# A third result group's last stage moved behind the last block's sums, and the last half's copies shared by two engines

## The chip, the cores and the metric

The kernel runs on one core of one Trainium2 chip. The metric is the device time of one execution in microseconds (us). The engines named here are TensorE (PE in the profile; its weight loads are listed apart as PEld), VectorE (DVE), ScalarE (ACT), GpSimd (POOL) and SyncE (SP), which only issues transfers here. TensorE writes its results to PSUM, from where ScalarE or VectorE copy them to SBUF.

## The reference

Two long convolutions over a sequence of 2048 steps and 448 channels are computed and mixed by a gate. Cut to what matters:

```python
# A: state-space model; K is a kernel of 2048 taps for each channel
P = jnp.exp(logdA[:, :, None] * l[None, None, :])
K = jnp.einsum("dn,dnl,dn->dl", Cc, P, dB).real
y = irfft(rfft(up) * rfft(Kp))[:, :, :L]        # causal convolution
a = y + u * Dskip
# B: a short convolution (4 taps), times v, then a long one
kv = k_shift * v
b = q * (irfft(rfft(kv) * rfft(ssm_k)) + kv * ssm_D)   # q is u as well
# gate
g = sigmoid((x * gate_w).sum(-1, keepdims=True))
return g * a + (1 - g) * b
```

The sum over the 256 modes of each channel that gives K, and the convolutions, are most of the work.

## The kernel before

The channels are cut in four groups (112 columns in all, 28 in a group, NC). Each convolution is a transform in stages, done with matmuls: *spread* (stage C), *transform* (stage 2), a pointwise product of the two transforms (*products*, or *last* for the last group), then *stage_a* and *stage_b* back. The kernel K of the A groups is built in eight blocks, two to a group: VectorE builds tables TQ and TP of powers, TensorE sums them over the modes (224 matmuls into `pk`), and `gather` and `spread` bring the sums into the form that the transform needs.

The copy functions:

```python
    def evac(dst, src, i=0):
        return nc.scalar.copy(dst, src)

    def evac_two(dst, src, i=0):
        if i == 0:
            nc.scalar.copy(dst, src)
        else:
            V.tensor_copy(dst, src)
```

The stages that the end of the kernel uses:

```python
def spread(nc, psum, W, zs, cols, groups, evac, room=8, tag="ps", at=0):
    for whs in groups:
        pt = psum.tile([P, room, 128], f32, name="ps_c", tag=tag)
        for i, wh in enumerate(whs):
            x = cols(wh)
            for r in range(2):
                nc.tensor.matmul(pt[64 * r:64 * r + 64, i, :], lhsT=x, rhs=W[:, 128 * r:128 * r + 128], start=True, stop=True,
                                 tile_position=(0, 64 * r))
        n = len(whs)
        evac(zs[:].rearrange("p k (g c) -> p (k g) c", g=4)[:, :, at + whs[0]:at + whs[0] + n], pt[:, 0:n].rearrange("p i kg -> p kg i"))
# ...
def transform_half(nc, psum, W, zs, evac, half):
    for kk in range(2):
        pt = psum.tile([P, 2, 512], f32, name="ps_2", tag="ps")
        for i in range(16):
            k = 16 * kk + i
            nc.tensor.matmul(pt[:, i // 8, (i % 8) * 56:(i % 8 + 1) * 56], lhsT=W[:, k].rearrange("p r s -> p (r s)"),
                             rhs=half_of(zs, k, k + 1, half), start=True, stop=True)
        for i in range(2):
            k0 = 16 * kk + 8 * i
            evac(half_of(zs, k0, k0 + 8, half), pt[:, i, 0:448].rearrange("p (k c) -> p k c", c=CB), i)


def stage_a_half(nc, psum, U, R, terms, evac, half):
    for j in range(half * CB, half * CB + CB, 7):
        pt = psum.tile([P, 8, 128], f32, name="ps_a", tag="ps")
        for i in range(7):
            for n, t in enumerate(terms):
                nc.tensor.matmul(pt[:, i, :], lhsT=t[:].rearrange("p k (g c) -> p (k g) c", g=4)[:, :, j + i],
                                 rhs=R[:, 128 * n:128 * n + 128], start=(n == 0), stop=(n == 1))
        evac(U[:, :, :, j:j + 7].rearrange("p r b c -> p (r b) c"), pt[:, 0:7].rearrange("p i rb -> p rb i"))
# ...
def stage_b(nc, psum, G, U, consume, banks=2):
    n = 16 * banks
    for b0 in range(0, 64, n):
        pt = psum.tile([P, banks, 512], f32, name="ps_b", tag="ps")
        for i in range(n):
            b = b0 + i
            o = pt[:, i // 16, (i % 16) * NC:(i % 16 + 1) * NC]
            for r in range(2):
                nc.tensor.matmul(o, lhsT=G[:, b, r].rearrange("p g a -> p (g a)"), rhs=U[:, r, b], start=(r == 0), stop=(r == 1))
        consume(b0, n, pt[:, :, 0:448])
```

`pt` with the tag "ps" is one of three PSUM tiles of two banks each. The end of a block of K, where the sums stand, and the gathering:

```python
# ... KGen.block: tables TQ and TP on VectorE ...
        q512 = mult([TQ[:, 18:19]], 512)
        p64 = mult([TP[:, 0:4]], 64)
        add(TQ, 20, q512)
        add(TP, 8, p64)
        p64 = mult([TP[:, 4:8]], 64)
        back(8, 16)
        add(TP, 12, p64)
        back(0, 8)
        self.last = chain[0]
        with self.tc.high_priority(offset=100000):
            pt = self.pk[:, 0:448].rearrange("p (n b) -> p n b", b=32)
            for hw in range(CB):
                for hf in range(2):
                    for c in range(2):
                        for g in range(4):
                            m = (hf * 4 + g) * CB + hw
                            r0 = TP[:, 0, c, m:m + 1]
                            rhs = bass.AP(r0.tensor, r0.offset, [list(r0.ap[0]), [32 * M + (1 - 2 * c) * M, 2], [2 * M, 16]])
                            nc.tensor.matmul(pt[32 * g:32 * g + NQ, hw, :].rearrange("p (i j) -> p i j", i=2),
                                             lhsT=TQ[:, :, c, m], rhs=rhs, start=(hf == 0 and c == 0),
                                             stop=(hf == 1 and c == 1), tile_position=(0, 32 * g))
            S = self.pool.tile([P, 32, CB], bf16, name="kg_S")
            self.summed = evac(S[:], pt.rearrange("p n b -> p b n"))
# ... KGen.gather: 57 small matmuls in two halves; each half is copied with
#     evac to KT, and both halves use the same PSUM bank ...
```

A block with its spread, and what happens to a group's result:

```python
    def block(j):
        H = j // 2
        if j and j % 2 == 0:
            tb.chunk(H, kg.mid)
        if KA[H] is None:
            KA[H] = qt([P, 32, 4 * NC], "zsK")
        S = kg.block(j, evac, kvl if j == 0 else None)
        with tc.high_priority(offset=100):
            KT = kg.gather(j, S, evac)
            at = (j % 2) * CB
            cols = lambda c: KT[:, :, c]
            if j >= NBLK - 2:
                spread(nc, psum, WcK, KA[H], cols, [range(0, 7), range(7, 14)], evac, at=at)
            else:
                spread(nc, psk, WcK, KA[H], cols, [range(0, 4), range(4, 8), range(8, 11), range(11, 14)], evac, 4, "ps_g", at)
# ...
    def epilogue_A(H):
        def consume(b0, n, pt):
            t = kgp.tile([P, 32, NC], bf16, name="ept")[:, 0:n]
            V.tensor_tensor(out=t.rearrange("p (i b) c -> p i b c", b=16), in0=pt.rearrange("p i (b c) -> p i b c", b=16),
                            in1=gt[:, b0:b0 + n].rearrange("p (i b) -> p i b", b=16).unsqueeze(3).to_broadcast([P, n // 16, 16, NC]), op=ALU.mult)
            V.tensor_tensor(out=window(b0, n, H), in0=t, in1=window(b0, n, H), op=ALU.add)
            if H == NQG - 1:
                store(b0, n, 0, 112)
        return consume

    y2 = []

    def hold_y(H):
        y2.append(hqt([P, 64, NC], "y2"))

        def consume(b0, n, pt):
            evac(y2[0][:, b0:b0 + n].rearrange("p (i b) c -> p i (b c)", b=16), pt)
        return consume

    def mix_y(H):
        for b0 in (0, 32):
            y = y2[0][:, b0:b0 + 32]
            yp = y.rearrange("p b (n t) -> p b n t", t=2)
            V.tensor_tensor(out=yp, in0=yp, in1=gb[:, b0:b0 + 32].unsqueeze(2).to_broadcast([P, 32, NC // 2, 2]), op=ALU.mult)
            V.tensor_tensor(out=window(b0, 32, H), in0=y, in1=window(b0, 32, H), op=ALU.add)
```

One step of the main sequence, and the end of the program:

```python
    def step(c, n, j):
        kind, H = n
        if kind == "B":
            KB[H] = spread_in(skc.pop(H))
            XB[H] = spread_in(kv_cols(H))
        else:
            XA[H] = spread_in(u_cols(H))
        with tc.high_priority(offset=300000):
            U = stage_a(nc, psum, qp, R, terms[c], evac)
        if kind == "B":
            transform(nc, psum, W2, KB[H], evac)
            transform(nc, psum, W2, XB[H], evac)
        else:
            transform(nc, psum, W2, XA[H], evac)
        with tc.high_priority(offset=200000):
            stage_b(nc, psum, G, U, (hold_y if c == ("A", NQG - 2) else epilogue_A if c[0] == "A" else epilogue_B)(c[1]))
        if kind == "B" and H + 1 < NQG:
            skc[H + 1] = sk_cols(H + 1)
        block(j)
        if kind == "B":
            with tc.high_priority(offset=200000):
                terms[n] = products(nc, *swapped(KB[H], kg.summed), XB[H])
        else:
            XA[H] = swapped(XA[H], kg.summed)
        if kind == "A" and H < NQG - 1:
            transform(nc, psum, W2, KA[H], evac)
            with tc.high_priority(offset=200000):
                terms[n] = products(nc, *XA[H], KA[H])
# ...
    for l in range(0, 112, 8):
        nc.tensor.matmul(pg[:], lhsT=ones[:], rhs=ug[:, :, l:l + 8], start=(l == 0), stop=(l == 104))
    gt = wp.tile([P, 64], f32, name="gt")
    V.tensor_reduce(out=gt[:], in_=pg[:], op=ALU.add, axis=mybir.AxisListType.X)
    nc.scalar.activation(gt[:], gt[:], ACT.Sigmoid)
    gb = wp.tile([P, 64, 2], bf16, name="gb")
    V.tensor_copy(gb[:], gt[:].unsqueeze(2).to_broadcast([P, 64, 2]))
    og = wp.tile([P, 64, 2], bf16, name="og")
    V.tensor_scalar(out=og[:], in0=gt[:].unsqueeze(2).to_broadcast([P, 64, 2]), scalar1=-1.0, scalar2=1.0, op0=ALU.mult, op1=ALU.add)
    pairs = lambda t: t[:].rearrange("p b (n t) -> p b n t", t=2)
    V.tensor_tensor(out=pairs(ug), in0=pairs(uu), in1=og[:].unsqueeze(2).to_broadcast([P, 64, 56, 2]), op=ALU.mult)

    seq = [("B", 0), ("B", 1), ("B", 2), ("A", 0), ("B", 3), ("A", 1), ("A", 2), ("A", 3)]
    for j in range(NBLK - 1):
        step(seq[j], seq[j + 1], j)

    U = qt([P, 2, 64, NC], "U")

    def last(half):
        for k0 in (0, 16):
            for t in XA[3][::-1]:
                V.tensor_tensor(out=half_of(t, k0, k0 + 16, half), in0=half_of(t, k0, k0 + 16, half), in1=half_of(KA[3], k0, k0 + 16, half), op=ALU.mult)

    transform_half(nc, psum, W2, KA[3], evac, 0)
    last(0)
    block(NBLK - 1)
    transform_half(nc, psum, W2, KA[3], evac_two, 1)
    stage_a_half(nc, psum, U, R, XA[3], evac, 0)
    last(1)
    mix_y(NQG - 2)
    stage_a_half(nc, psum, U, R, XA[3], evac, 1)
    stage_b(nc, psum, G, U, epilogue_A(3), 1)
```

`tc.high_priority` and the order of the program decide how a scheduler puts the instructions of one engine in order; that order is fixed when the kernel is built. `swapped` issues the transfer that writes a copy `zsS` of `zs` with its two halves of partitions exchanged.

## Time and profile before

| | before |
|---|---|
| time, median of 3 | 325.49 us (325.31 to 325.81) |
| span of the profiled execution | 323.5 us |
| VectorE busy | 277.2 us (86%) |
| ScalarE busy | 243.2 us (75%) |
| TensorE busy, matmuls / weight loads | 225.5 us (70%) / 197.4 us (61%) |
| mean granted TensorE clock | 0.8 |
| last stage B begins | 308.08 us |
| last instruction of VectorE ends | 313.6 us |

The profile is of one execution. A line of the timeline has the start (us from the span's start), the length in us, the engine, the line of the kernel, the operation, what it writes and reads, the shapes, and how many instructions are merged in it; in brackets stands the time that the engine was idle before it and what ended that. The chain of work that ended last is followed back from the last instruction, at each step to what released it; "issue" there is time in which an engine waited for nothing that the profile shows. L565 is the line of the function `evac`, L569 and L571 are those of `evac_two`, so the tile's name tells which copy it is. The granted clock is a share of full speed.

### The profile page before, as it was taken

To read this page: it belongs to the slowest core of one execution; us is meant where nothing else is said; L and a number is where in the kernel's file an instruction comes from. 1 tells how busy PE (TensorE), PEld (TensorE's weight loads), DVE (VectorE), ACT (ScalarE), POOL (GpSimd) and SP (SyncE) were. 2 spreads that over 40 slices of the span, in tenths; PEclk is the share of its full clock that TensorE was granted. 3 is DMA by queue.
4 is the path that set the end of the run, shared out by engine and by line. 5 is a ranking of instruction groups with operands and counts; after the bars stand their busy time and mean duration, and the time that the engine had idled before them with its cause. 6 is when DMAs were issued, how large, how long until landed. Compare 5 with 4: busy or idle time off the path is not lost.

```text
span 323.5 us, 11944 instructions
## 1 busy us (share of the span) xinstructions
PE 225.5 (70%) x5286; PEld 197.4 (61%) x5286; DVE 277.2 (86%) x571; ACT 243.2 (75%) x395; POOL 34.6 (11%) x129
## 2 busy tenths in 40 slices
PE   0498617737278678699997857999774779966740
PEld 0144607237167568588886846998674678865740
DVE  7999999967999899979999998988999889942450
ACT  3655888779991799998989999689989474936600
POOL 9400002912000009000000000000000000000000
PEclk9999855796758767967997975899998559995765
DMA  6889999730000530050040015004000500040048
GB/s 129 137 188 152 165 164 168 239 59 0 2 0 4 117 57 3 5 158 2 4 102 19 4 45 116 3 4 97 22 2 4 115 3 4 12 108 2 2 91 140
DMA packets 53740, 21.41 MB, mean 66 GB/s; under 512 B 49080, under 2 KB 52024, under 8 KB 53688
## 3 DMA queue, kind: packets, MB, share of 16 engines
q1 hardware_dynamic: 48936, 19.47, 31.6%
q10 hardware_dynamic: 4560, 1.15, 2.0%
q8 instruction: 41, 0.67, 0.9%
q14 instruction: 11, 0.09, 0.1%
q0 software_dynamic: 192, 0.03, 0.1%
HBM read 10.09 MB, written 3.21 MB: 41 GB/s over the span
## 4 chain that ended last, share of the span: by engine, by line
ACT 39%; PE 26%; SPq 14%; DVE 9%; POOL 4%; issue 3%; DMA 3%; ACTq 0%; DVEq 0%; POOLq 0%
ACT zs L565 12%; PE ps_b L279 7%; PE pk L371 6%; ACT ET L481 6%; ACT U L565 5%; ACT zsK L565 5%; PE ps_c L215 5%; SPq L634 4%; POOL skraw L592 4%; PE ps L227 3%; SPq L587 3%; PE ps_a L265 3%; ACT ET L493 3%; SPq L631 2%; ACT ET L511 2%
## 5 line engine op out<-in xcount | busy, mean ns | idle before, releaser
L565 ACT CAST zs<-ps_c 128x1024 bf16<-128x1024 f32 (+1 forms) x48 | 42.5, 940 | 4.8 <-PE ps_c L215 4.7
L227 PEld LDWEIGHTS <-s_W 128*128 128x128 bf16 x480 | 34.4, 118 | 16.7 <-issue 14.2
L318 DVE TENSOR_TENSOR kg_P<-kg_TQ,ET 128x896 bf16<-128x896 bf16 (+1 forms) x64 | 43.8, 705 | 0.3
L565 ACT CAST zs<-ps 128x896 bf16<-128x896 f32 x48 | 41.4, 929 | 1.6 <-PE ps L227 1.5
L227 PE MATMUL ps<-zs,s_W 128*128 128x112 bf16 x384 | 32.2, 252 | 12.2 <-ACT zs L565 6.3
L371 PE MATMUL pk<-kg_TP,kg_TQ 128*21 128x32 bf16 x1792 | 30.3, 238 | 8.5 <-issue 6.3
L371 PEld LDWEIGHTS <-kg_TQ 128*21 128x21 bf16 x1792 | 27.8, 121 | 10.3 <-issue 9.6
L265 PE MATMUL ps_a<-sa_R,zs 128*128 128x128 bf16 x196 | 29.0, 240 | 6.8 <-ACT U L565 4.5
L592 POOL TENSOR_TENSOR skraw<-skraw,dB 128x28 bf16<-128x28 bf16 x4 | 23.3, 5816 | 94.9 <-DMA skraw<-in_B_ssm_k_dram 94.9
L565 ACT CAST U<-ps_a 128x1024 bf16<-128x1024 f32 (+2 forms) x32 | 29.3, 947 | 3.5 <-PE ps_a L253 1.8
L318 DVE TENSOR_TENSOR kg_P<-kg_TP,ET 128x1792 bf16<-128x1792 bf16 (+1 forms) x32 | 30.8, 963 | 0.0
L279 PEld LDWEIGHTS <-sb_G 128*128 128x128 bf16 x1024 | 27.9, 99 | 3.9 <-issue 3.6
L279 PE MATMUL ps_b<-U,sb_G 128*128 128x28 bf16 x1024 | 28.1, 179 | 2.9 <-ACT U L565 1.3
L265 PEld LDWEIGHTS <-zsS 128*128 128x128 bf16 x196 | 26.2, 153 | 5.2 <-issue 5.2
L265 PE MATMUL ps_a<-sa_R,zsS 128*128 128x128 bf16 x196 | 28.5, 239 | 0.0
L265 PEld LDWEIGHTS <-zs 128*128 128x128 bf16 x196 | 26.2, 152 | 2.6 <-DVE zs L286 1.7
L323 DVE TENSOR_TENSOR kg_TQ<-kg_P 128x896 bf16<-128x896 bf16 (+2 forms) x64 | 27.7, 442 | 0.2
L493 ACT ACTIVATE ET<-ks_ph 128x448 bf16<-128x448 int16 x40 | 23.8, 603 | 5.0 <-DVE ks_ph L489 4.0
L565 ACT CAST zsK<-ps_c 128x512 bf16<-128x512 f32 (+2 forms) x28 | 22.1, 798 | 7.0 <-PE ps_c L215 6.9
L215 PE MATMUL ps_c<-WcK,kg_KT 128*64 128x128 bf16 x224 | 19.9, 305 | 9.1 <-ACT zsK L565 5.8
L655 PE MATMUL ps_v<-kvt,scratch 128*128 128x448 bf16 x64 | 16.3, 387 | 13.5 <-DVE kvt L651 13.1
L215 PE MATMUL ps_c<-Wc,kv 128*64 128x128 bf16 x224 | 15.6, 321 | 14.1 <-DVE kv L680 7.8
(141 smaller groups left out, 481.4 us busy)
## 6 DMA issues: line engine op xcount, KB each, us to landing
zsS<-zs SPq DMA_DIRECT2D x16, 448.0 KB, 5.6
kt<-in_B_k_dram SPq DMA_DIRECT2D x16, 112.0 KB, 4.3
skraw<-in_B_ssm_k_dram SPq DMA_DIRECT2D x16, 112.0 KB, 3.6
vt<-in_B_v_dram SPq DMA_DIRECT2D x4, 448.0 KB, 6.8
uu<-in_A_u_dram SPq DMA_DIRECT2D x4, 448.0 KB, 8.7
xfd<-ks_hold SPq DMA_DIRECT2D x2, 672.0 KB, 6.9
ks_xf<-xfd SPq DMA_DIRECT2D x3, 336.0 KB, 3.0
out_dram<-ug SPq DMA_DIRECT2D x8, 112.0 KB, 4.8
```

What stands on the lines that cost most here:

```text
L215: nc.tensor.matmul(pt[64 * r:64 * r + 64, i, :], lhsT=x, rhs=W[:, 128 * r:128 * r + 128], start=True, stop=True, tile_position=(0, 64 * r))
L227: nc.tensor.matmul(pt[:, i // 4, (i % 4) * n:(i % 4 + 1) * n], lhsT=W[:, k].rearrange("p r s -> p (r s)"), rhs=zs[:, k], start=True, stop= ...
L265: nc.tensor.matmul(pt[:, i, :], lhsT=t[:].rearrange("p k (g c) -> p (k g) c", g=4)[:, :, j + i], rhs=R[:, 128 * n:128 * n + 128], start=(n ...
L279: nc.tensor.matmul(o, lhsT=G[:, b, r].rearrange("p g a -> p (g a)"), rhs=U[:, r, b], start=(r == 0), stop=(r == 1))
L318: put(V.tensor_tensor(out=P4[:, i:i + m].rearrange("p n v c m -> p n v (c m)"), in0=in0, in1=in1, op=ALU.mult))
L323: put(V.tensor_tensor(out=T[:, dst:dst + v.shape[1] // 2].rearrange("p n v m -> p (n v) m"), in0=v[:, :, 0], in1=v[:, :, 1], op=ALU.add))
L371: nc.tensor.matmul(pt[32 * g:32 * g + NQ, hw, :].rearrange("p (i j) -> p i j", i=2), lhsT=TQ[:, :, c, m], rhs=rhs, start=(hf == 0 and c == 0),
L481: ex = nc.scalar.activation(dst, x, ACT.Exp, scale=float(e))
L493: sn = nc.scalar.activation(dst.rearrange("p b c m -> p b (c m)"), low16(ph[:].rearrange("p b c m -> p (b c m)")).rearrange("p (b x) -> p ...
L565: return nc.scalar.copy(dst, src)
L592: nc.gpsimd.tensor_tensor(out=raw[:, :, 0], in0=raw[:, :, 0], in1=dB[:, H * NC:(H + 1) * NC], op=ALU.add)
L655: nc.tensor.matmul(pt[:, i, 0:448], lhsT=ident, rhs=t[:, n, 4 * i:4 * i + 4, :].rearrange("p b l -> p (b l)"), start=(n == 0), stop=(n == 3))
```

## The change

In the kernel before, the third A group's stage B (of `("A", 2)`) is done in the step of block 6; its result is copied out of PSUM by ScalarE in bf16 (`hold_y`), and VectorE multiplies it by the gate in bf16 and adds it much later in the program (`mix_y`). In the kernel after, all of that stage B is ordered behind the sums of the last block on TensorE (`summed` puts an order on that engine alone, no wait between engines), and its result goes through `epilogue_A`, as those of the other groups do: VectorE multiplies out of PSUM and adds. This is meant to give TensorE work while the sums are copied and gathered, and to take copies from ScalarE. Besides, the copies of the last block's spread and of the last group's stage A go by turns to ScalarE and VectorE (`evac_two`), where ScalarE did all of them. The steps of the end are written out, with priorities of their own, in an order in which the second half's transform stands behind the first half's stage A.

The diff, cut to its core:

```diff
-def spread(nc, psum, W, zs, cols, groups, evac, room=8, tag="ps", at=0):
+def spread(nc, psum, W, zs, cols, groups, evac, room=8, tag="ps", at=0, then=None):
 ...
-        evac(zs[:]..., pt[:, 0:n].rearrange("p i kg -> p kg i"))
+        evac(zs[:]..., pt[:, 0:n].rearrange("p i kg -> p kg i"), whs[0] % 2)
 ... stage_a_half
-        evac(U[:, :, :, j:j + 7]..., pt[:, 0:7].rearrange("p i rb -> p rb i"))
+        evac(U[:, :, :, j:j + 7]..., pt[:, 0:7].rearrange("p i rb -> p rb i"), j % 2)
 ... stage_b
+                if then is not None:
+                    then(mm)
 ... KGen.block
-                            nc.tensor.matmul(pt[32 * g:32 * g + NQ, hw, :]...
+                            self.sums = nc.tensor.matmul(pt[32 * g:32 * g + NQ, hw, :]...
 ...
+    def summed(mm):
+        after(tc, mm, kg.sums)
 ... block: split into kg.block and place; in place:
+        end = j == NBLK - 1
-                spread(nc, psum, WcK, KA[H], cols, [range(0, 7), range(7, 14)], evac, at=at)
+                spread(nc, psum, WcK, KA[H], cols, [range(0, 7)], evac_two if end else evac, at=at)
+                spread(nc, psum, WcK, KA[H], cols, [range(7, 14)], evac_two if end else evac, at=at)
 ... hold_y and mix_y are gone, and the copy gb of the gate in bf16
-            stage_b(nc, psum, G, U, (hold_y if c == ("A", NQG - 2) else epilogue_A if c[0] == "A" else epilogue_B)(c[1]))
+            stage_b(nc, psum, G, U, (epilogue_A if c[0] == "A" else epilogue_B)(c[1]))
 ...
-    for j in range(NBLK - 1):
+    for j in range(NBLK - 2):
         step(seq[j], seq[j + 1], j)
 ... the step of block 6, written out:
+    tb.chunk(3, kg.mid)
+    KA[3] = qt([P, 32, 4 * NC], "zsK")
+    XA[3] = spread_in(u_cols(3))
+    with tc.high_priority(offset=300000):
+        U2 = stage_a(nc, psum, qp, R, terms["A", 2], evac)
+    transform(nc, psum, W2, XA[3], evac)
+    S6 = kg.block(NBLK - 2, evac)
+    place(NBLK - 2, S6)
+    XA[3] = swapped(XA[3], kg.summed)
 ... the end:
-    transform_half(nc, psum, W2, KA[3], evac, 0)
-    last(0)
-    block(NBLK - 1)
-    transform_half(nc, psum, W2, KA[3], evac_two, 1)
-    stage_a_half(nc, psum, U, R, XA[3], evac, 0)
-    last(1)
-    mix_y(NQG - 2)
-    stage_a_half(nc, psum, U, R, XA[3], evac, 1)
+    S7 = kg.block(NBLK - 1, evac)
+    stage_b(nc, psum, G, U2, epilogue_A(2), 2, summed)
+    transform_half(nc, psum, W2, KA[3], evac, 0)
+    last(0)
+    with tc.high_priority(offset=150000):
+        place(NBLK - 1, S7)
+    U = qt([P, 2, 64, NC], "U")
+    stage_a_half(nc, psum, U, R, XA[3], evac_two, 0)
+    with tc.high_priority(offset=150000):
+        transform_half(nc, psum, W2, KA[3], evac_two, 1)
+    with tc.high_priority(offset=150000):
+        last(1)
+    stage_a_half(nc, psum, U, R, XA[3], evac_two, 1)
     stage_b(nc, psum, G, U, epilogue_A(3), 1)
```

## The prediction

> **What bounds the kernel now.** I read the page first, then the last 40 us of the chain of work that ended last, then each engine's timeline there. On the page VectorE is the busiest engine:
>
> ```profile
> PE 225.5 (70%) x5286; PEld 197.4 (61%) x5286; DVE 277.2 (86%) x571; ACT 243.2 (75%) x395; POOL 34.6 (11%) x129
> ```
>
> The share hides two stages. From 265 to 285 us VectorE is busy 19.4 of 20.0 us with the tables of block 7 (TQ, TP); from 285 to 300 us it is busy 4.0 of 15. The change touches nothing ahead of about 270 us: compared instruction by instruction, the built kernels have the same order up to the sums of block 6 on every engine, but for one small copy (gb) that goes. So only the end counts. The chain from 284 us on, columns start, length, what:
>
> ```profile
> 285.00 1.53 PE pk L371 x73
> 286.53 1.38 issue
> 287.90 2.12 PE pk L371 x115
> 290.02 1.33 issue
> 291.36 0.23 PE pk L371 x2
> 291.59 0.88 PE ps L241 x16
> ...
> 292.54 1.84 ACT zsK L565 x4
> 294.39 0.45 ACT kg_KT L565
> ...
> 294.88 0.94 PE ps_g L412 x25
> ...
> 295.84 0.55 ACT kg_KT L565
> ...
> 296.44 1.11 PE ps_c L215 x14
> ...
> 297.57 2.12 ACT zsK L565 x2
> ...
> 299.72 0.92 PE ps L241 x16
> ```
>
> Nobody is full here: it is a relay between TensorE and ScalarE. The sums pk of block 7 are 224 matmuls, of which two stops called "issue" take 2.7 us. Then the sums are copied (kg_S), gathered, copied (kg_KT) twice over, spread, copied by ScalarE in two pieces (2.12 us), and transformed. After that follow the products, stage A of the second half, its two U copies (305.91, 2.13 us, both ScalarE) and the last stage B at 308.08; from there the four epilogues and the store take 15.4 us to the span's end at 323.5. The last tables end at 283.49 + 1.09 = 284.58 on VectorE, and TensorE is free at about 284.9, so the sums start on both almost at once.
>
> The third A group's stage B lies ahead of the sums, where nothing waits for its place:
>
> ```profile
> 279.83 3.36 PE L279 MATMUL ps_b<-U,sb_G 128*128 128x28 bf16 x128 [0.26 <-ACT zs L565]
> 281.68 0.97 ACT L565 CAST y<-ps_b 128x896 bf16<-128x896 f32 x1
> 283.23 0.91 ACT L565 CAST y<-ps_b 128x896 bf16<-128x896 f32 x1 [0.58 <-PE ps_b L279]
> 284.50 1.15 DVE L762 TENSOR_TENSOR y<-y,gb 128x896 bf16<-128x896 bf16 x2
> ```
>
> The reader is to see that its copies y and mixing run while ScalarE and VectorE have no other urgent work: what is removed there was almost free.
>
> [...] the second run of pk above has exactly 128, and each stop costs 1.3 to 1.4 us[...]. [...] in the stretch view the granted clock falls from 1.00 to 0.50 at 290 us, after the stops, and is back at 303.5. [...] the multiplication ept out of PSUM takes 1.08 us for 128x896, one in SBUF 0.62. [...] the shared copies overlap at 301.29 (VectorE) and 301.41 (ScalarE).
>
> **Part 1, the stage B moved behind the sums.** Removed ahead of the sums: 3.4 us of TensorE and two copies of 0.9 us on ScalarE. The sums then wait for VectorE alone: 284.65 in place of 284.93, a gain of 0.3 us. More comes from the first stop. As many instructions are moved behind the sums as make one block (128 pairs), so the block edges keep their places in the sums, after pair 95 and pair 223. The block that starts 33 pairs ahead of the sums began in the kernel before at about 283.0, together with the zsS transfer (115 to 300 GB/s from 282.8 to 287), and its successor was there at 287.90, 4.9 us later. Without such traffic it took 3.46 us (287.90 to 291.36). In the new order these 33 pairs are the last 5 of a transform and the 28 spreads of block 6, so the edge is crossed near 279 to 281, ahead of the zsS transfer, and the first stop of 1.38 us should vanish. The second remains: edge at 284.65 + 1.6 = 286.2, next block at 286.2 + 3.46 = 289.7, or up to 1 us later because the transfer still runs until 287. With 0.3 us for the last pair and the hand-over, the kg_S copy starts at about 290.0 in place of 291.63: 1.6 us gained.
>
> **Part 2, from the kg_S copy (time 0) to the last stage B.** Before, 308.08 - 291.63 = 16.45 us. In the new order TensorE's queue behind the sums reads 46 stage B, 17 gather, 46 stage B, 40 gather, 36 stage B, 32 transform (first half), 28 spread, 28 stage A, 32 transform (second half), 28 stage A, 128 stage B. A stage B pair takes 3.36/128 = 26 ns. Laid out: 46 pairs to 1.1; gather to 1.8; 46 pairs to 3.0; gather to 3.8; 36 pairs to 4.8; transform to 6.1 (1.0 to 1.7 us by clock); spread to 8.0. Before, the spread ended at 298.35, time 6.7: the chain loses 1.3 us on TensorE, since of 3.4 us added only about 2 fill waits for copies.
> VectorE meanwhile has two epilogues of group 2 (2 x (1.08 + 0.62) = 3.4 us, ending about 6.5), then four products of the first half (4 x 0.54, which cannot end before 8.6 to 9.1, as the first-half copies on ScalarE end at 7 to 7.8), and only then its piece of the spread (a copy of about 1.05 us): 9.7 to 10.2. Sharing was to save 1.05 us on this pair; behind the products VectorE saves nothing.
> Next TensorE does 28 stage A matmuls of the first half ahead of the second transform. They wait for the products (8.6 to 9.1) and take 1.8 us at full clock and 2.9 at half (63 and 105 ns each, both seen from 301 to 304): the transform starts at 10.4 to 12.0 where it started at 299.72 - 291.63 = 8.1. From its start to the end of the products I get 4.5 us warm (5.0 before, at half clock), as its copies are on two engines again; stage A with U copies on two engines 3.1 in place of 3.3. The last stage B so starts at 18.0 with full clock all along and 19.9 with half clock. TensorE is nearly full from 0 to 8, so I expect the clock back between 4 and 8, and take 18.5: 2.05 us lost.
>
> **Part 3, the end.** Stage B with one bank, four epilogues and store are unchanged: 15.4 us.
>
> Sum: -1.6 + 2.05 = +0.45, thus 325.49 + 0.45 = 325.9 us.
>
> **Rivals.** (a) The filling works: TensorE stays at full clock through the whole tail, and the two U and spread copies run side by side without VectorE's queue in the way. For it: TensorE stood for about 9 of 20 us in this stretch, and VectorE for 6.8 and 5.5 us at a time. Then the tail is 16.5 to 17 and the time 323.9 to 324.5. (b) The first stop stays, since the fetch is slow for a reason other than the traffic, and the clock stays at half: no gain of 1.4 us, tail 19.9. That makes 325.5 - 0.3 + 3.4 = 328.6. Against it: the fetch took 3.46 us where no transfer ran. (c) TensorE's queue does not bind, and ScalarE does, as it did between 292.54 and 294.83: with the y copies gone and half of the last copies moved away it has less, so this would give 325 or below; I think it weak, since ScalarE already waited in the kernel before.
>
> **Range and chances.** The sums' end is uncertain by about 1.3 us, the clock by 1.9, VectorE's queue by about 1. Together a range of 323.8 to 328.2 should hold 8 times in 10. 2% is 6.5 us, more than all terms together: faster 0.01, same 0.97, slower 0.02.
>
> **What would show it.** Right: pk from about 284.65 with one stop instead of two, the kg_S copy near 290.0; L281 matmuls between the two gathers; the second half's transform 10 to 12 us behind kg_S, waiting for stage A of the first half; VectorE's copy of ps_c behind the first-half products. Wrong: a transform that starts 8 to 9 us behind kg_S (the queue order then cost nothing, and the kernel gains), two stops in pk, or a start of pk that moved because VectorE's tables ended at another time than 284.58. A difference ahead of 270 us would break the whole working.

## The result and the profile after

The changed kernel takes 328.07 us (median of 4 runs, 327.43 to 328.78), the kernel before 325.46 in the same series: a ratio of 1.0079, interval [1.0056, 1.0102]. Measured again in a later series: 328.60 us (6 runs), 1.0072 [1.0049, 1.0095]. The change makes the kernel 0.8% slower.

The profile after has a span of 325.7 us, 2.2 more than before. On its page VectorE is busy for 4.4 us more than before and ScalarE for 5.5 us less:

```profile
PE 221.8 (68%) x5286; PEld 193.8 (59%) x5286; DVE 281.6 (86%) x573; ACT 237.7 (73%) x390; POOL 26.1 (8%) x129
```

The order of instructions is the same up to the sums of block 6, and there the two profiles wander against each other: the copies kg_S of the seven blocks before the last come between 0.74 us earlier and 1.10 us later than in the profile before. The last tables end at 285.29, 0.71 later than before, which is of that size, so I measure from the tables' end and not from the span's start. In this kernel L569 is the line of `evac`, and L573 and L575 are those of `evac_two`; lines shown with an experiment are those of its own kernel.

The chain of work that ended last, from the sums of block 7 on (start, length, what, count):

```profile
285.35 3.53 PE pk L375 x202
288.88 1.47 issue
290.35 0.23 PE pk L375 x2
290.58 1.25 PE ps_b L281 x46
291.84 0.68 PE ps_g L416 x11
292.52 1.34 PE ps_b L281 x46
...
299.75 2.01 PE ps_a L255 x28
...
301.79 1.14 DVE U L575
302.93 1.04 DVE zsK L575 x2
...
306.16 3.09 PE ps_a L255 x28
...
310.42 0.98 PE ps_b L281 x32
```

Two things are to be seen. At the top the sums have one stop where they had two. Below, TensorE does the moved stage B (L281) between the gathers, with hardly a gap; but from 295.80 on the chain goes through VectorE again and again (an epilogue, the four products, then U and zsK here), where in the kernel before it was a relay between TensorE and ScalarE. VectorE's own timeline in the middle of that stretch:

```profile
299.61 1.13 DVE L575 CAST zsK<-ps_c 128x896 bf16<-128x896 f32 x1
```

The copy of the last spread (ps_c), which the second transform needs, comes behind the first half's products and ends at 300.74. The transform starts at 301.58, right behind the first half's stage A, and its own copies come behind a copy of U (301.79 in the chain). TensorE then has nothing to do until the products are through, a long stop ahead of the second half's stage A:

```profile
301.58 0.99 PE L243 MATMUL ps<-zsK,s_W 128*128 128x56 bf16 x32
...
306.16 0.33 PE L255 MATMUL ps_a<-sa_R,zs 128*128 128x128 bf16 x1 [3.59 <-DVE zs L822]
```

And the stretches of 2 us there (length; busy us and instructions of PE, PEld, DVE, ACT, POOL; granted clock; share and GB/s of DMA):

```profile
304.00:306.00 2.00, 0.00 (x0) 0.00 (x0) 2.00 (x4) 0.00 (x0) 0.00 (x0) 0.89 0.00 0
306.00:308.00 2.00, 1.84 (x18) 1.84 (x19) 0.10 (x1) 0.09 (x1) 0.00 (x0) 0.50 0.00 0
```

From 304 to 306 TensorE does nothing at all and VectorE is full; then the clock is at half, just when the 28 matmuls of stage A come, and they take 3.09 us instead of 2.01 for the first half's.

### The tail in three terms

The rest of the document reads every kernel by the same points: the start of the copy kg_S; the start of the second half's transform; the end of the last product (zs, VectorE); the start of the last stage B. They are read from the timelines of TensorE, ScalarE and VectorE. "To kg_S" is counted from the end of the last tables. "Stop" is how long TensorE stood ahead of the second half's stage A. The copy kg_S in the kernel before and after:

```profile
291.63 0.53 ACT L565 CAST kg_S<-pk 128x448 bf16<-128x448 f32 x1 [5.31 <-PE pk L371]
290.62 0.53 ACT L569 CAST kg_S<-pk 128x448 bf16<-128x448 f32 x1 [6.15 <-PE pk L375]
```

| kernel | to kg_S | kg_S to transform | transform to products' end | products' end to last stage B | tail | stop | time, us |
|---|---|---|---|---|---|---|---|
| before | 7.05 | 8.09 | 4.99 | 3.37 | 16.45 | 0.71 | 325.46 |
| after | 5.33 | 10.96 | 4.52 | 4.32 | 19.80 | 3.59 | 328.07 |
| after, second profile | 5.65 | 12.24 | 4.90 | 4.36 | 21.50 | 3.50 | 328.60 |
| e1, transform ahead of stage A | 5.73 | 10.44 | 5.13 | 3.23 | 18.80 | 1.17 | 326.48 |
| e2, copies by one engine | 5.72 | 12.10 | 5.11 | 4.45 | 21.66 | 4.04 | 328.99 |
| e3, only copies shared | 6.69 | 7.70 | 5.01 | 3.23 | 15.94 | 1.15 | 325.29 |
| e4, no transfer | 4.78 | 6.57 | 4.99 | 3.37 | 14.93 | 1.05 | 322.72 |
| e5, stage B left out | 5.59 | 9.00 | 4.52 | 4.45 | 17.97 | 3.59 | 325.65 |
| e6, only moved, mixed one by one | 4.97 | 12.90 | 4.55 | 3.35 | 20.80 | 1.62 | 329.43 |
| e6b, only moved | 5.34 | 9.14 | 4.53 | 3.36 | 17.03 | 1.63 | 324.48 |
| e7, moved and shared | 5.40 | 8.36 | 4.66 | 3.23 | 16.25 | 0.54 | 325.09 |
| b1, moved into the gaps | 5.53 | 7.58 | 5.02 | 3.78 | 16.38 | none | 322.87 |
| b2, another such order | 5.67 | 6.91 | 4.60 | 3.23 | 14.74 | none | 322.94 |
| b3, b2 with the block edge moved | 3.65 | 8.65 | 4.56 | 3.24 | 16.45 | none | 323.24 |

The terms are those of one profile each, the times are medians of 2 to 22 runs in four series, in which the kernel before took 325.42 to 325.85; the ratios below are to the kernel before in the same series. A profile is one run. At equal points ahead of the tail two profiles differ by up to about 1 us, and the two tails of the kernel after by 1.7, so a row's sum does not give its time to a tenth, and differences of under 2 us between two tails need the times beside them.

### The profile page after: what moved, and what is told of

It is laid out like the page before. It is cut to its first block, busy times and chain, and to the rows that moved or that the text cites. A ratio compares the mean times of both kernels' runs of the same rounds, so it can differ in the third digit from the quotient of the medians.

```text
span 325.7 us, 11943 instructions
## 1 busy us (share of the span) xinstructions
PE 221.8 (68%) x5286; PEld 193.8 (59%) x5286; DVE 281.6 (86%) x573; ACT 237.7 (73%) x390; POOL 26.1 (8%) x129
## 3 DMA queue, kind: packets, MB, share of 16 engines
q10 hardware_dynamic: 4560, 1.15, 2.0%
HBM read 10.09 MB, written 3.21 MB: 41 GB/s over the span
## 4 chain that ended last, share of the span: by engine, by line
ACT 33%; DVE 27%; PE 22%; SPq 6%; DMA 5%; issue 3%; DVEq 0%; ACTq 0%
ACT zs L569 10%; PE ps_b L281 7%; ACT ET L485 6%; DVE kg_P L322 5%; PE pk L375 5%; ACT zsK L569 4%; PE ps L229 3%; PE ps_a L267 3%; ACT U L569 3%; DVE zsS L290 2%; DVE zs L290 2%; ACT ks_mag L485 2%; PE ps_c L215 2%; ACT ET L497 2%; DMA vt<-in_B_v_dram 2%
## 5 line engine op out<-in xcount | busy, mean ns | idle before, releaser
L569 ACT CAST zs<-ps_c 128x1024 bf16<-128x1024 f32 (+1 forms) x48 | 42.6, 941 | 4.0 <-PE ps_c L215 4.0
L569 ACT CAST zs<-ps 128x896 bf16<-128x896 f32 x48 | 41.1, 927 | 2.4 <-PE ps L229 2.4
L229 PEld LDWEIGHTS <-s_W 128*128 128x128 bf16 x480 | 31.1, 110 | 18.6 <-issue 16.5
L229 PE MATMUL ps<-zs,s_W 128*128 128x112 bf16 x384 | 29.2, 235 | 14.0 <-ACT zs L569 8.5
L375 PE MATMUL pk<-kg_TP,kg_TQ 128*21 128x32 bf16 x1792 | 30.1, 238 | 10.4 <-issue 5.8
L267 PE MATMUL ps_a<-sa_R,zs 128*128 128x128 bf16 x196 | 29.8, 243 | 6.2 <-ACT U L569 4.7
L281 PE MATMUL ps_b<-U,sb_G 128*128 128x28 bf16 x1024 | 28.8, 181 | 3.3 <-issue 1.4
L281 PEld LDWEIGHTS <-sb_G 128*128 128x128 bf16 x1024 | 28.2, 100 | 4.4 <-issue 2.7
L267 PE MATMUL ps_a<-sa_R,zsS 128*128 128x128 bf16 x196 | 29.2, 241 | 0.0
L569 ACT CAST U<-ps_a 128x1024 bf16<-128x1024 f32 (+1 forms) x28 | 25.2, 914 | 2.6 <-PE ps_a L267 2.5
L215 PE MATMUL ps_c<-WcK,kg_KT 128*64 128x128 bf16 x224 | 19.9, 298 | 9.0 <-ACT zsK L569 5.7
L215 PEld LDWEIGHTS <-kv 128*64 128x64 bf16 x224 | 15.3, 220 | 15.3 <-DVE kv L684 8.8
L569 ACT CAST zsK<-ps_c 128x512 bf16<-128x512 f32 (+2 forms) x26 | 20.0, 778 | 5.7 <-PE ps_c L215 5.7
```

Of the source, the lines that this page charges most:

```text
L215: mm = nc.tensor.matmul(pt[64 * r:64 * r + 64, i, :], lhsT=x, rhs=W[:, 128 * r:128 * r + 128], start=True, stop=True, tile_position=(0, 64 ...
L229: nc.tensor.matmul(pt[:, i // 4, (i % 4) * n:(i % 4 + 1) * n], lhsT=W[:, k].rearrange("p r s -> p (r s)"), rhs=zs[:, k], start=True, stop= ...
L281: mm = nc.tensor.matmul(o, lhsT=G[:, b, r].rearrange("p g a -> p (g a)"), rhs=U[:, r, b], start=(r == 0), stop=(r == 1))
L375: self.sums = nc.tensor.matmul(pt[32 * g:32 * g + NQ, hw, :].rearrange("p (i j) -> p i j", i=2), lhsT=TQ[:, :, c, m], rhs=rhs, start=(hf = ...
```

## The experiments

The theory: the change gains at the sums and loses at the end, and it loses because its order puts VectorE's and TensorE's work for the first half ahead of what the second half waits for. The rivals: the moved matmuls and epilogues themselves cost the time; sharing the copies costs it.

### The transform ahead of stage A

On the kernel after, the first half's stage A is ordered behind the second half's transform:

```diff
+        turned = transform_half(nc, psum, W2, KA[3], evac_two, 1)
-    stage_a_half(nc, psum, U, R, XA[3], evac_two, 0)
-        transform_half(nc, psum, W2, KA[3], evac_two, 1)
+    stage_a_half(nc, psum, U, R, XA[3], evac_two, 0, lambda mm: after(tc, mm, turned))
```

> The kernel after, with the second half's transform put ahead of the first half's stage A on TensorE. My theory, that the place of stage A in TensorE's queue costs twice (it delays the transform, and TensorE then stands while VectorE multiplies, so that its clock falls): the transform starts about 10.2 us behind the kg_S copy in place of 11.0, the 28 stage A matmuls of the second half run at full clock (1.9 us in place of 3.0), and the last stage B begins 17.9 to 18.3 us behind kg_S in place of 19.8; 326.2 us, 1.9 less than the kernel after. Rival, that VectorE's queue binds: the last stage B stays at 19.3 or later, 327.7 us or more.

Measured: 326.48 us (20 runs), ratio to the kernel before 1.0023 [1.0008, 1.0038]; that is 1.6 to 2.1 below the two medians of the kernel after. The chain:

```profile
301.12 0.94 PE ps L243 x16
...
306.31 2.00 PE ps_a L256 x28
```

The order is worth most of the loss, but not in the place where I had looked for it: the transform starts 10.44 us behind kg_S, only 0.52 earlier than after, since it still waits for VectorE's copy of ps_c. What is gained is the last term, 3.23 in place of 4.32: stage A of the first half now lies in the gap, TensorE stands 1.17 us instead of 3.59, the clock is at 1.00 from 306 to 310, and the second half's stage A takes 2.00 us.

### The copies by one engine

On the kernel after, the order on TensorE held as it is:

```diff
-                spread(..., evac_two if end else evac, at=at)
+                spread(..., evac, at=at)
-    stage_a_half(nc, psum, U, R, XA[3], evac_two, 0)
+    first = stage_a_half(nc, psum, U, R, XA[3], evac, 0)
-        transform_half(nc, psum, W2, KA[3], evac_two, 1)
+        transform_half(nc, psum, W2, KA[3], evac_two, 1, lambda mm: after(tc, mm, first))
-    stage_a_half(nc, psum, U, R, XA[3], evac_two, 1)
+    stage_a_half(nc, psum, U, R, XA[3], evac, 1)
```

> The kernel after, with the copies of the last spread and of both stage A halves all on ScalarE as in the kernel before, and TensorE's order as in the kernel after. My theory, that sharing these copies is worth almost nothing in this order, as VectorE's piece stands behind the first half's products and as the second U copy waits for slow stage A matmuls anyway: 327.6 to 328.6 us. Rival, that the sharing saves one copy of 1.05 us on the spread and one on U: 329.1 to 330.2 us.

Measured: 328.99 us (6 runs), ratio 1.0083 [1.0060, 1.0107]. Against 1.0079 and 1.0072 for the kernel after the intervals overlap: sharing does not cause the loss, and if it is worth anything in this order, it is less than about 1 us, which these intervals would not show. The stop is there too (4.04 us), and stage A takes 3.22 us, 0.107 us from one matmul to the next, the pace that the kernel after has at a clock of 0.50:

```profile
308.20 3.22 PE ps_a L258 x28
```

### Only the copies shared

On the kernel before: the last block's spread and the second half's U copies by turns.

```diff
-        evac(zs[:]..., pt[:, 0:n].rearrange("p i kg -> p kg i"))
+        evac(zs[:]..., pt[:, 0:n].rearrange("p i kg -> p kg i"), whs[0] % 2)
-                spread(..., evac, at=at)
+                spread(..., evac_two if j == NBLK - 1 else evac, at=at)
-    stage_a_half(nc, psum, U, R, XA[3], evac, 1)
+    stage_a_half(nc, psum, U, R, XA[3], evac_two, 1)
```

> The kernel before with the other part of the change alone: the second piece of the last spread and the second U copy of the last stage A go to VectorE. My theory, that VectorE is idle at both places in the kernel before: the spread's pieces end together, 1.0 us earlier, and the U copies 0.2 to 1.0 us earlier by the clock; the last stage B 14.6 to 15.4 us behind kg_S in place of 16.45; 324.0 to 324.9 us. Rival, that TensorE at half clock takes what the copies give: 16.2 us and 325.5.

Measured: 325.29 us (22 runs), ratio 0.9994 [0.9981, 1.0006]: no difference that shows. The first term is 0.39 and the last 0.14 shorter than before, which such a measurement cannot tell from nothing. The tail of 15.4 us or less that I had expected did not come (15.94).

### The sums without the transfer

On the kernel before, the last group's exchanged table (zsS) is made by two copies in the core in place of the transfer that exchanges its halves. The exchange of the halves of partitions is left out, so the fourth group gets other values; only the time is read.

```diff
+            if H == NQG - 1:
+                swap = qt([P, 32, 4 * NC], "zsS")
+                for k0 in (0, 16):
+                    evac(swap[:, k0:k0 + 16], XA[H][:, k0:k0 + 16])
+                XA[H] = (XA[H], swap)
```

> The kernel before, where the last group's zsS is written by ScalarE out of zs in place of the transfer (the exchange of the two halves of partitions is left out, so group 4 of the output is another). My theory, that the first stop in the sums is a fetch of instructions held up by the traffic of that transfer: the first stop of 1.38 us shrinks to below 0.3, the second stays at 1.3, the kg_S copy comes about 5.7 us behind the end of the tables in place of 7.05, and the time is 324.1 us. Rival, that the fetch takes its time whatever the traffic: two stops of 1.3 to 1.4 us and 325.5 us.

Measured: 322.72 us (2 runs), ratio 0.9906 [0.9882, 0.9930]. The sums on TensorE's timeline:

```profile
285.87 3.52 PE L371 MATMUL pk<-kg_TP,kg_TQ 128*21 128x32 bf16 x222
290.32 0.23 PE L371 MATMUL pk<-kg_TP,kg_TQ 128*21 128x32 bf16 x2 [0.93 <-issue]
```

The stop behind pair 95 is gone without anything having been moved: 222 matmuls run through, and kg_S comes 4.78 us behind the tables in place of 7.05. The first stop needs the transfer. That carries the prediction's first part, where the same stop vanished because its edge was crossed ahead of the transfer (in the kernel after the packet of instructions that belongs to this edge starts at 280.04, the zsS transfer at 283.70). The tail is shorter too (14.93 against 16.45), and the clock stays at 1.00 until about 296.7, where it was at half from 290 on in the kernel before; that the one comes from the other is not shown: in e3, with the transfer and both stops, the clock stayed at 1.00 until 292.35.

The DMA records of the traces show the fetch itself. They have single packets of 16 KB of the kind "instruction": 41 in the kernels before and after, with 5286 pairs of weight load and matmul on TensorE, 40 in e5 with 5158 pairs and 42 in b3 with 5394, one for 128 to 129 pairs each time; and between the two stops of the kernel before stand 128 matmuls on the timeline (the chain lists 115 of them). In all the profiles each stop in the sums, and the one that b3 moved, ends 1.2 to 1.7 us after such a packet has landed. In the kernel before the packets start at 285.33 and 288.99 and land 0.88 and 0.93 us later, and the stops end at 287.90 and 291.36. In the kernel after, the packet starts at 287.88, while the zsS transfer ends at 287.93; of the ten other profiles with one stop, b3's among them, it starts within 0.13 us of that transfer's end in nine, and 0.32 us behind it in e1. In e4, without a transfer, it starts at 287.97, about 0.6 us behind the edge by an estimate from the pace of the sums (285.87 + 95 x 16 ns = 287.4). In the kernel after 287.88 is 1.0 us behind the edge by the same estimate (285.35 + 95 x 16 ns = 286.87), so I put what the transfer adds to the second fetch there at some tenths of a microsecond.

### Stage B left out

On the kernel after, the third group's stage B and its mixing are left out; the order of everything else stays.

```diff
-    stage_b(nc, psum, G, U2, epilogue_A(2), 2, summed)
-    transform_half(nc, psum, W2, KA[3], evac, 0)
+    transform_half(nc, psum, W2, KA[3], evac, 0, summed)
```

> The kernel after with the third A group's stage B and its mixing left out (that quarter of the channels keeps only its B part), all else in the order of the kernel after. My theory, that half of the tail's loss lies in the order of the steps and in the clock, and not in the added matmuls: the last stage B still 16.5 to 18.5 us behind kg_S (19.8 with stage B, 16.45 in the kernel before), 323.5 to 325.6 us. Rival, that the 128 added pairs in TensorE's queue are the whole loss: 15.5 to 16.4 us behind kg_S and 322.5 to 323.4 us.

Measured: 325.65 us (14 runs), ratio 0.9989 [0.9970, 1.0009]. The chain:

```profile
296.92 2.80 PE ps_a L258 x28
...
304.12 3.22 PE ps_a L258 x28
```

With the moved work taken out altogether, the tail still takes 17.97 us where the kernel before, which has none of it there either, takes 16.45. The same stop of 3.59 us is there, and stage A behind it takes 3.22 us. So of the tail's loss of 3.35 us (19.80 - 16.45) about 1.5 come with the order (and the shared copies) alone and about 1.8 only when the stage B is in it. That split is of these profiles; the second profile of the kernel after, with a tail of 21.50, would make the second part larger.

### Only the move, in the order of before

On the kernel before: stage B of the third group goes behind the sums, in pieces of 46, 46 and 36 matmuls around the two gathers; its result is still copied by ScalarE (`hold_y`), and the first half's transform stays right behind the sums.

```diff
+            moved = stage_b_steps(nc, psum, G, held[0], hold_y(NQG - 2), 2, then)
+            take(moved, 46)
+            between = lambda: take(moved, 46)
-            KT = kg.gather(j, S, evac)
+            KT = kg.gather(j, S, evac, then, between)
+            if j == NBLK - 1:
+                take(moved, 36)
```

A first build of it left the order within the gathers to the scheduler:

> The kernel before with one part of the change alone: the third A group's stage B ordered behind the last block's sums; its result still copied out by ScalarE and mixed by VectorE in bf16, and all other steps in the order of the kernel before. My theory, that the move itself wins at the sums what it loses on TensorE's queue, and that the kernel after loses by its other order: kg_S 5.4 us behind the end of the tables in place of 7.05, the last stage B 17.7 to 18.5 us behind kg_S in place of 16.45, 325.1 to 325.9 us. Rival, that the moved stage B is the whole loss: 19.5 us behind kg_S or more, 327 us or more.

Measured: 329.43 us (6 runs), ratio 1.0104 [1.0085, 1.0123]. It does not answer the question, because gather and stage B went one by one (TensorE's timeline, one row a matmul):

```profile
292.08 0.22 PE L414 MATMUL ps_g<-kg_S,ga_sel 128*32 128x112 bf16 x1
292.23 0.19 PE L279 MATMUL ps_b<-U,sb_G 128*128 128x28 bf16 x1
292.35 0.22 PE L414 MATMUL ps_g<-kg_S,ga_sel 128*32 128x112 bf16 x1
```

A pair takes 0.27 us from start to start, so 17 pairs some 4.7 us, where 16 gather matmuls in a row take 0.73 us (the chain below) and 17 of stage B 17 x 26 ns = 0.44. (The granted clock of e6's profile does not go above 0.85, where the others reach 1.00; its run was still the fastest of the six, 328.32.) With the three pieces in fixed runs:

> As the only-moved kernel, but the matmuls of stage B and of the gather not mixed one by one: 46, 17, 46, 40 and 36 as in the kernel after, behind the first half's transform. My theory: the sums gain 1.7 us (kg_S 5.4 us behind the tables), TensorE's queue loses 1.2 to 2.7 (last stage B 17.6 to 19.2 us behind kg_S); 325.0 to 326.7 us. Rival, that stage B behind the sums costs all of its 3.4 us and more wherever it stands: 19.8 us or more behind kg_S and 327.2 us or more.

Measured: 324.48 us (21 runs), ratio 0.9967 [0.9953, 0.9980]. The chain:

```profile
289.65 0.93 PE ps L241 x32
290.59 1.19 PE ps_b L293 x46
291.78 0.73 PE ps_g L433 x16
```

The move alone is faster than the kernel before, and than I had expected. It has the gain at the sums (5.34 against 7.05, 1.71 us), and its tail is 17.03, only 0.58 longer than before. The first half's transform is done first, so that the first products are through by 293.5, before the spread is there, and nothing stands ahead of the copies of ps_c.

### Moved and shared, in the order of before

The last kernel with the shared copies of "Only the copies shared" added.

> Both parts of the change (stage B behind the sums, the second pieces of the last spread and of the last U copies on VectorE), in the order of steps of the kernel before and with the y copies of the kernel before. My theory, that the change fails by its order alone: at least as fast as the kernel with stage B moved only, the last stage B 16.0 to 17.0 us behind kg_S, 323.6 to 324.6 us. Rival, that stage B behind the sums and the sharing don't go together, since VectorE's mixing comes between: 325.5 us or more.

Measured: 325.09 us (12 runs), ratio 0.9979 [0.9959, 0.9999]. Both parts of the change, without its new order, make a kernel that is no slower than before. Between this one and the kernel after lie 3.55 us of tail (19.80 - 16.25). VectorE's copy of ps_c comes early here, and the second transform starts right behind it:

```profile
299.62 1.28 PE L241 MATMUL ps<-zsK,s_W 128*128 128x56 bf16 x32 [1.19 <-DVE zsK L596]
```

### A better order

If order is the cause, a better one should keep the gain at the sums and shorten the tail. On the kernel after, with TensorE's and VectorE's orders fixed: the second transform ahead of the first half's stage A, and stage B in three pieces (26 and 38 pairs around the first gather, 64 between the two halves of stage A):

> The kernel after with the order of the tail fixed so that each matmul of the moved stage B stands where TensorE waits: 26 pairs during the kg_S copy, 38 during the first kg_KT copy, 64 during the last products; the first half's transform during the second kg_KT copy; the second half's transform ahead of all stage A; the spread in three pieces, the middle one on VectorE. My theory: the sums keep the 1.7 us gained, and the last stage B begins 14.2 to 15.5 us behind kg_S in place of 16.45 before and 19.8 after; 321.6 to 323.2 us. Rival, that stage B in the chain costs its time anyway: 17 us and more, 324.5 us or more.

Measured: 322.87 us (6 runs), ratio 0.9926 [0.9901, 0.9951]. Faster than both kernels, but its tail is 16.38, longer than I had expected. The chain tells why:

```profile
294.90 3.21 ACT zsK L597 x6
...
298.15 1.65 PE ps L243 x32
```

Six copies in a row on ScalarE hold the second transform, which then takes 1.65 us at a clock of 0.54 (mean from 298 to 300), where it takes 0.99 at 1.00 in the kernel after. The next version does the first half's transform between the two gathers, so that its copies lie apart from those of the spread, keeps the spread in b1's pieces of 5, 5 and 4, puts stage B in pieces of 32, 32 and 64, and fixes ScalarE's order too:

```diff
+    def between():
+        held.extend((turn(0, 0), turn(0, 1)))
+        turned(0, 0, held[0], evac_a)
 ...
+    spread(..., [range(0, 5)], evac_a, at=CB, then=q)
+    spread(..., [range(5, 10)], evac_v, at=CB, then=q)
+    spread(..., [range(10, 14)], evac_a, at=CB, then=q)
```

> A second order for the tail: gather first behind the sums, the first half's transform during the first kg_KT copy, the moved stage B in runs of 32 pairs during the second kg_KT copy, 32 during the spread's copies and 64 during the last products; ScalarE's and VectorE's orders fixed too. My theory: kg_S 5.5 us behind the tables as in the kernel after, the last stage B 14.0 to 15.6 us behind kg_S; 321.0 to 322.6 us. Rival, that three PSUM tiles or VectorE's own work (9 us of it from the first products to the last) hold it up as in the kernel in the gaps: 16 us and more, 322.6 us or more.

Measured: 322.94 us (6 runs), ratio 0.9906 [0.9884, 0.9928]. The chain:

```profile
298.63 2.01 PE ps_a L255 x28
300.64 1.59 PE ps_b L870 x64
...
302.26 2.01 PE ps_a L255 x28
```

The moved stage B fills the time in which the kernel after had its stop of 3.59 us; both stage A take 2.01 us, what the first half's takes in the kernel after at a clock of 1.00. This kernel, whose tail is 14.74, has all of the change's matmuls behind the sums and all its epilogues out of PSUM on VectorE, and its second transform starts 6.91 us behind kg_S. That it is a better kernel than before is measured; which of its fixed orders does how much is not, since they were changed together, and b1 and b2 do not differ by more than their intervals.

### The block edge moved

The remaining stop in the sums is at a count of instructions. 108 matmuls with no use, added at the start of the program in b2, should move it out of the sums:

```diff
+    shift = psum.tile([P, 2, 512], f32, name="ps_s", tag="ps")
+    for i in range(108):
+        nc.tensor.matmul(shift[:, 0, 0:28], lhsT=ident, rhs=ident[:, 0:28], start=True, stop=True)
```

> The same kernel with 108 small matmuls (128x28) added at the start, where TensorE waits for VectorE; their result is not used. They shift the edges of the blocks of 128 pairs by 108, so that the second edge falls 20 pairs behind its old place, 19 pairs behind the end of the sums and no longer one pair ahead of it. My theory, that the second stop is a fetch of instructions: the sums run through without a stop, kg_S comes 3.9 to 4.3 us behind the tables in place of 5.5, the stop of about 1 us stands behind the gather or is hidden by the kg_KT copy; 1.0 to 1.7 us less than the same kernel without them, 319.5 to 321.3 us. Rival, that the stop belongs to the sums and not to the count of instructions: a stop of 1.5 us inside the sums stays and the time is the same, or 2 to 3 us more for the added matmuls.

Measured: 323.24 us (6 runs), ratio 0.9917 [0.9893, 0.9940]. The chain:

```profile
285.91 3.58 PE pk L377 x190
...
289.51 0.54 ACT kg_S L575
...
290.83 1.63 issue
292.46 1.25 PE ps L881 x31
```

The stop goes where the count says: the sums run through, kg_S comes 3.65 us behind the tables in place of 5.67, and TensorE stops in the transform behind the gather instead. The gain of 1.0 to 1.7 us that I had expected did not come, since that transform is on the path as well. Here too the fetch waits for the transfer: its packet starts at 290.22, the zsS transfer ends at 290.23, and the edge was crossed at about 287.8 by the same kind of estimate (285.91 + 115 x 16 ns).

## Why the prediction was right and wrong

It said 325.9 us, and 323.8 to 328.2 as a range; measured were 328.07. That it would be within 2% of the time before, and a little slower rather than faster, was right; the size, 0.4 us, was too small by 2.2.

**The sums, right.** Predicted: the first stop vanishes, the second stays, 1.6 us gained. The profile has one stop, and kg_S comes 1.72 us sooner behind the tables. The cause, the transfer that delays the fetch of the next block, is shown by e4 (kg_S 4.78 us behind the tables in place of 7.05) and the packets, and the counting of edges by b3 (3.65 in place of 5.67). The second fetch, which the sum has at 3.46 us as one without a transfer, waited for the transfer too (287.88 and 287.93). That the tables themselves ended 0.71 us later was not in the sum, though the prediction names it as a sign of being wrong. The change is not shown to do it: VectorE is 0.71 us later already at 277.69 (276.98 before), ahead of where the moved stage B stood, and such a wander shows at every block.

**The tail up to the second transform, right.** 46 pairs, gather, 46, gather, 36 came as laid out. The transform of the first half started 5.0 us behind kg_S (4.8 predicted), the spread ended at 8.2 (8.0), the products at 9.1 (8.6 to 9.1), VectorE's copy of ps_c at 10.1 (9.7 to 10.2), and the second transform started at 10.96, inside 10.4 to 12.0; with 4.5 and 3.1 behind it, the 18.5 that I took leaves 18.5 - 4.5 - 3.1 = 10.9. From there to the end of the products it took 4.52 (4.5).

What I had less right is who holds the transform. I named stage A ahead of it in TensorE's queue, and that was indeed the last to end, but only 0.84 us behind VectorE's copy of ps_c (301.58 - 300.74). e1 took it away, and it brought 0.52 us. The next to hold it is that copy, in line behind epilogues and products of the first half, which I had listed and then not named as a bound. e7 shows that the same matmuls and the same sharing need not hold it (8.36 us). It differs from the kernel after in at least three things at once, the place of the first half's transform, the first half's stage A, and `hold_y` in place of the epilogue out of PSUM; beyond the 0.52 they were not taken apart. b2 shows that the epilogue out of PSUM alone does not forbid an early start (6.91 us).

**The failed term: "stage A with U copies on two engines 3.1".** It measured 4.32 us, 1.22 more. That is nearly all by which the tail, 19.80, exceeds the 18.5 of the prediction. The term took full clock for the second half's stage A, on the words that the clock would be "back between 4 and 8". So it was: from 295.31, 4.7 us behind kg_S, at the end of 3.41 us in which TensorE was busy throughout (291.90 to 295.31, clock 0.50). But I stopped following TensorE there. My own layout had the first half's stage A done before the transform, and so nothing left for TensorE between the end of the transform and the end of the products. It stood 3.59 us, the clock went down again, and 28 matmuls took 3.09 us instead of 2.0. That the prediction's case "with half clock", 19.9 us, lies so near the 19.80 is luck: by its own figures its 1.9 us are the first half's transform (1.0 to 1.7) and stage A (1.8 to 2.9), and these took 0.99 and 2.01 us, at a clock of 1.00. The table shows what such a stop costs in both directions: with stops of 3.5 to 4.0 us the last term is 4.32 to 4.45 (after twice, e2, e5), with stops of 0.5 to 1.6 us it is 3.23 to 3.37 (before, e1, e3, e4, e6, e6b, e7).

The long stop and the fall of the clock go together: it fell at 305.55, and in the 3.41 us ahead of that TensorE was busy for 0.43 us. But it fell after fuller stretches too. In the kernel before the clock fell at 289.87, ahead of the second stop in the sums and not after both, as the prediction reads it, and in the 3.42 us ahead of that TensorE was busy for 2.04. In b1 it fell at 298.17 after 2.68 us busy of 3.42, and the second transform ran at half clock behind a stop of only 0.67 us.

One thing of the clock I had overlooked: in each profile it changes only at points that lie 3.41 us, or a multiple of that, apart (before: 265.98, 289.87, 303.52, 310.35; after: 285.07, 288.48, 291.90, 295.31, 305.55, 308.96), and from run to run these points lie elsewhere in the kernel. What a stop does to the clock may then depend on where among these points it falls, and not on its length alone; no run tested that.

**The rest of the difference.** Of 2.2 us (328.07 - 325.9), 1.3 are the longer tail, nearly all of it this term, and 0.6 the later kg_S (290.62 against 290.0). The end took 15.3 us against 15.4. Some 0.4 is left because the profiled runs are not the median ones: 328.07 is 2.4 above its profile's span, 325.49 is 2.0 above that of before.

**The rivals.** (a), the filling works, failed for this kernel. The same move in the old order came out where (a) put it (e6b: 324.48, tail 17.03), but not in (a)'s way: nothing is shared there, and the clock was at half from 291.05 to 294.46. (a) also has TensorE stand for too long: from 285 to 305 us of the kernel before it is busy for 13.63 us, so it stood for about 6 us of 20 and not 9. (b) had both of its parts wrong or half wrong: the first stop did go, and the clock did not stay at half, but was back at full by 295.31 and fell again at 305.55; its time of 328.6 was near by accident. (c), ScalarE binds, finds nothing in the kernel after, where ScalarE waits up to 4.70 us for TensorE in the tail; in b1 it was the bound for 3.21 us.

**What stays open.** In the second profile of the kernel after the tail is 21.50 us, with the clock at half from 284.38 to 298.03. The points at which the clock changes lie elsewhere there (it fell 1.57 us ahead of the tables' end, in the first profile 0.22 us), which may be why; it was not tested. What share of such a stretch TensorE must be busy to keep the clock does not come out of the profiles either; the runs of this kernel lie between 327.43 and 329.89.

## What to carry to other kernels

Work that fills an engine's gap is worth what the order around it lets it be: the same 128 matmuls behind the sums made the kernel 0.2 to 0.3% faster with the first half's transform done first (e7, e6b, both with the result copied out by ScalarE) and 0.8% slower with it done behind them. When a step is moved, follow each engine's queue to the end of the path, and ask for every copy what stands ahead of it and for every gap whether anything is left to put there. A long gap on TensorE was paid twice here, once as itself (3.59 us) and once in the clock of the matmuls behind it (3.09 us in place of 2.01), so of two orders the one that keeps some work for the last gap is to be preferred.

## What the runs showed of the hardware that I had not expected

- Matmuls of the gather (weights of 128x32) and of stage B (128x128), one by one, take 0.27 us a pair (e6, clock 0.85); in runs of their own 46 ns (0.73/16, e6b, clock 0.50) and 26 ns each (3.36/128, the kernel before, clock 1.00). For 17 pairs that is 4.7 us in place of 1.2.
- The stop in the sums belongs to a count of instructions: 108 useless matmuls moved it out of the sums and into the next step, at about its old length (1.63 us in b3; 1.83 in b2). Without the transfer that ran ahead of them, one of the two stops was gone and the other was 0.93 us (e4). With it, the packet of instructions started only when the transfer ended in the kernel after (287.88 and 287.93); in the kernel before that of the first stop started in its midst (285.33; the transfer ran from 282.98 to 288.09).
- In each of the four profiles in which TensorE stood for 3.5 to 4.0 us ahead of the second half's stage A, that stage ran at half clock or its pace (0.107 us from one matmul to the next): 28 matmuls in 3.09 to 3.22 us in place of 2.01. The clock changed only at points 3.41 us, or a multiple of that, apart (305.55 and 308.96 in the kernel after).
